# First pole tables copied within SBUF, later poles behind the first products, three groups' layer norm statistics on ScalarE

## Chip, core and metric

The kernel runs on one core of a Trainium2 chip. Its time is the device time of one execution in microseconds (us); the median of three runs is given, and one further execution was taken with the hardware profiler. The engines are TensorE (PE; its weight loads are PEld), VectorE (DVE), ScalarE (ACT), GpSimd (POOL) and SyncE (SP), which here only issues DMAs. SBUF and PSUM are the core's on-chip memories; DRAM is the chip's main memory.

## What is computed

One block with two halves. The input `x` is [2048, 576]; `c` gives six modulation rows by `silu(c) @ w_mod`. The first half is a long convolution along the sequence whose kernel comes from 576 x 128 complex poles; the second is a gated MLP with a spatial product.

```python
h = _layernorm(x) * (1 + ca) + sa
x = x + ga * _A_ref(h, A_re, A_im, B_re, B_im, C_re, C_im, log_dt, Dskip)
h = _layernorm(x) * (1 + cb) + sb
x = x + gb * _B_ref(h, w_in, w_sp, b_sp, w_out)
# in _A_ref, with dt = exp(log_dt):
P = jnp.exp((dt * (A_re + 1j * A_im))[:, :, None] * l)   # l = 0 .. 2047
K = einsum("dn,dnl,dn->dl", C, P, dt * B).real           # then FFT convolution of h with K
```

## The kernel before, in words

`ssm` is the first half, `Mlp` the second. Only the front of `ssm` is touched.

**Poles.** The powers of a pole are split into magnitude and angle. `poles(c0, c1, Q)` computes, for a chunk range of the 576 channels (chunk 0 alone, width 144, then chunks 1 to 3 together, width 432), the log magnitude per step `al`, the log weight `lw`, the angles `tau` and `tau64` and the phase `ph`. It is a generator (`run`) with five `yield`s: its caller decides when each of six segments is written out. Six products run on GpSimd (L211 to L216), the exponential, logarithms and arctangent on ScalarE, the rest on VectorE. `split3` cuts each fp32 result into three bf16 pieces that add up to it, and stores them in DRAM (`pa_d`, `pb_d`, `pc_d`). `poles_load` reads them back in another shape, 16 channels by 3 or 6 pieces on the partitions: the tables `lb` (al and lw), `lc` (tau), `la` (tau64 and ph).

**Ticks.** 36 groups of 16 channels run through a pipeline, one group a tick in a loop of 40 ticks. `e_unit` (every third tick, for three groups) multiplies `lb` with a constant selector `sel` on TensorE and takes exponentials on ScalarE (L386, L389). `t_unit` forms the angles from `lc` and `la`, rounds them with a ScalarE pass (L397) and two VectorE passes (L398, L400); `s_unit` takes sine and cosine (L405, L406); `p_unit` multiplies on VectorE two ticks after `t_unit` (L417 to L421); `kg_unit`, `d_unit` and `k1_unit` sum over the poles and transform. From tick 9 on the input side joins in: `u_load`, `u_unit`, `z_unit`, `v_unit`, and later `y_unit`. These use space that the front's pool `ep` gives back at tick 9.

**Modulation and layer norm.** `mod_load` and `mod_unit` (L312 to L324) form one modulation row each, into the tiles `gar`, `cga` and `sga` for the first half. x is handled in four groups of four blocks of 128 tokens. `ln_load` reads a group, `ln_stats` takes mean and variance with VectorE's bn_stats (L353, L354) and a reciprocal root of 11 operations of width 4 (`rsqrt`, L741 to L751), `ln_unit` normalizes one block with two VectorE passes (L363, L364), transforms it with four matmuls (L369), copies it out (L370) and stores it (L371). Two blocks are handled a tick, in ticks 0 to 7; the buffers `ln_x` are two, `st1o` two, `mpart` one.

**Order.** Instructions called through `V`, `A`, `G`, `T` and `S` are ordered for each engine by the tile framework's planner, which goes by its own estimates of when inputs are there. Calls through `mlp.tied` (class `Pin`, L132) are pinned: behind whatever was written before on the same engine. Pinning fixes the place in the engine's own order only; what is written later and is not pinned may still be moved ahead of it. All instructions pinned this way show line 132 or the line of the operation. Before the loop the loads go through a pinned `S`, in this order: poles0, c, w_mod 2, small, w_mod 1, w_mod 0, x group 0, sel, r1t 0, then, behind the first poles, their table loads, and after the first modulation units dsk, x group 1, r1t 1 and poles 1 to 3.

Of the kernel before, what the change touches and what calls it, by code (L numbers as in the profile page):

```python
# [18 lines left out]
D = 576  # L19
# [125 lines left out]
def ssm(tc, I, x1_d, consts_s, dram, mod_d, mlp):  # L145
# [5 lines left out]
    with ExitStack() as ctx:  # L151
# [26 lines left out]


        def poles(c0, c1, Q):  # L180
            w = 144 * (c1 - c0)

            def t(n, dt=F32):
                return ep.tile([128, 432], dt, name="t_" + n, bufs=1)[:, :w]

            todo = []

            def split3(src, dst, k):

                n = 3 // (c1 - c0)  # L190
                if not todo:
                    t_ = ep.tile([128, 3, 432], BF, name="pt")
                    todo.extend(t_[:, :, w * i:w * i + w] for i in range(n))
                pt = todo.pop(0)
                V.tensor_copy(pt[:, 0], src)
                q = t("sq")
                V.tensor_tensor(q, src, pt[:, 0], op=ALU.subtract)
                V.tensor_copy(pt[:, 1], q)
                V.tensor_tensor(pt[:, 2], q, pt[:, 1], op=ALU.subtract)
                for c in range(c0, c1):  # L200
                    Q.dma_start(dst[c, k:k + 3].rearrange("q (p f) -> p q f", p=128), pt[:, :, 144 * (c - c0):144 * (c - c0) + 144])

            raw = ep.tile([128, 7, w], F32, name="nat%d" % c0, bufs=1)
            for r in (slice(0, 3), slice(3, 7)):
# [3 lines left out]
            def run():  # L208
# [10 lines left out]
                V.tensor_tensor(al, dt, al, op=ALU.mult)  # L219
                split3(al, pb_d, 0)  # L220
                yield
# [18 lines left out]
                A.activation(lw, mx, AF.Ln)  # L240
                A.activation(q1, mn, AF.Square)
                A.activation(q1, q1, AF.Ln, bias=one)
                A.activation(ph, mn, AF.Arctan)
                V.scalar_tensor_tensor(lw, q1, 0.5, lw, op0=ALU.mult, op1=ALU.add)
                V.tensor_tensor(lw, lw, ldt, op=ALU.add)
                split3(lw, pb_d, 3)
                yield
# [11 lines left out]
                yield  # L259
                split3(tau, pc_d, 0)  # L260
                split3(tau64, pa_d, 0)
# [6 lines left out]
        lt = {}  # L268

        def poles_load(c, Q):  # L270
            for n, d_, k in (("lb", pb_d, 6), ("lc", pc_d, 3), ("la", pa_d, 6)):
                t_ = tb.tile([16 * k, 9, 128], BF, name=n)
                Q.dma_start(t_, d_[c].rearrange("q (c g n) -> (q c) g n", c=16, g=9))
                lt[n, c] = t_

# [71 lines left out]
        def ln_stats(i):  # L347
            x = x4s[i]
            bs = ep.tile([128, 4, 2, 6], F32, name="bs")
            mv = ep.tile([128, 4, 2], F32, name="mv")  # L350
            for b in range(4):
                for h in range(2):
                    V.bn_stats(bs[:, b, h], x[:, b, HC * h:HC * h + HC])  # L353
                V.bn_aggr(mv[:, b], bs[:, b])  # L354
            r = ep.tile([128, 4], F32, name="r")
            rsqrt(V, ep, r, mv[:, :, 1], 4)
            lns[i] = mv, r

        def ln_unit(b):
            i, j = divmod(b, 4)  # L360
            mv, r = lns[i]
            n = x4s[i][:, j]
            V.scalar_tensor_tensor(n, n, mv[:, j, 0:1], cga, op0=ALU.subtract, op1=ALU.mult)  # L363
            V.scalar_tensor_tensor(n, n, r[:, j:j + 1], sga, op0=ALU.mult, op1=ALU.add)  # L364
# [241 lines left out]
        ln_stats(1)  # L606
        sb = cs = None
        for tick in range(NG + 4):
# [1009 lines left out]
```

## Time and profile before

| | us |
|---|---|
| median of 3 runs (lowest, highest) | 1794.5 (1794.14, 1796.96) |
| profiled execution | 1798.62 |
| its span, first to last instruction | 1796.9 |
| PE, DVE, ACT, POOL busy in the span | 1695.7, 1128.8, 785.6, 224.0 |
| DVE, ACT busy from 42.5 to 161.5 us | 105.4, 82.4 |

Lines of a view read as: engine, source line, operation, tile written <- tiles read, shapes, count; then busy us, mean ns of one, and the idle time of the engine before them with what ended it ("<-DMA x" is a transfer into x, "<-ACT ft L397" ScalarE's result of line 397). In lines in order of time the first number is the start and the second the duration, in us from the span's start. "ACTq" and "SPq" are the engines' issuing of DMAs.

### The profile page before, as it was taken

The page shows a single profiled execution, that of the slowest core. Times are in us where ns is not written, and L with a number is a line of the kernel's source. Part 1 is how long each engine was busy: PE and PEld are TensorE (multiplying, and loading weights), DVE is VectorE, ACT ScalarE, POOL GpSimd, SP SyncE. Part 2 cuts the span into 40 slices and gives each one's busy share as a digit, 9 for nine tenths or more (in the row PEclk, how much of TensorE's full clock was granted, in tenths as well). Part 3 has the DMA queues.
Part 4 walks back from the last instruction along what each step waited for, and adds up shares of the span by engine and source line. Part 5 has one row for each costly group of instructions (what it writes and reads, how often), then busy time and mean ns, then how long its engine had stood idle before and what let it go on. Part 6 is the DMA issues. An engine that isn't in the chain of part 4 may idle for free.

```text
span 1796.9 us, 34078 instructions
## 1 busy us (share of the span) xinstructions
PE 1695.7 (94%) x14202; PEld 1197.6 (67%) x14202; DVE 1128.8 (63%) x2253; ACT 785.6 (44%) x1021; POOL 224.0 (12%) x350
## 2 busy tenths in 40 slices
PE   4687999996899999999999999999999999999999
PEld 1344555565455545877787777877778777887787
DVE  6987999857888997999784444474222265222322
ACT  4658999844476666555441322241111132011110
POOL 1321232342122211000000000000000000000000
PEclk8788999998899999999999999999999999999999
DMA  8457445779588788877564675562655472555520
GB/s 274 139 196 243 139 119 163 195 207 314 169 266 261 241 259 246 301 277 257 206 216 148 240 250 206 212 250 92 227 192 197 173 264 69 176 181 175 199 83 27
DMA packets 153034, 361.57 MB, mean 201 GB/s; under 512 B 24832, under 2 KB 68224, under 8 KB 150960
## 3 DMA queue, kind: packets, MB, share of 16 engines
q1 hardware_dynamic: 110272, 167.30, 29.4%
q0 software_dynamic: 33120, 153.95, 25.8%
q10 hardware_dynamic: 9488, 38.16, 5.3%
q8 instruction: 111, 1.82, 0.4%
q14 instruction: 43, 0.35, 0.1%
HBM read 256.86 MB, written 93.05 MB: 195 GB/s over the span
## 4 chain that ended last, share of the span: by engine, by line
PE 51%; DVE 16%; DMA 7%; issue 4%; ACT 4%; SPq 0%; POOL 0%; ACTq 0%; DVEq 0%; POOLq 0%
PE ps L1324 9%; PE ps L1359 8%; PE ps L1361 8%; PE ps L1360 8%; PE pz L132 3%; PE ps L1408 3%; PE ps L1409 3%; PE ps L1410 3%; DMA raw<-in_w_spT 2%; DVE zset L1066 2%; DVE gt L1373 2%; DMA z_d<-z 2%; ACT z L132 1%; DVE bsz L132 1%; PE pk L132 1%
## 5 line engine op out<-in xcount | busy, mean ns | idle before, releaser
L1359 PE MATMUL ps<-wsp,zset 128*128 128x256 f16 x2016 | 549.5, 273 | 2.8 <-DVE gt L1373 2.6
L1361 PE MATMUL ps<-wsp,zset 128*128 128x256 f16 x2016 | 549.5, 273 | 0.2 <-DVE zset L1066 0.2
L1360 PE MATMUL ps<-wsp,zset 128*128 128x256 f16 x2016 | 549.5, 273 | 0.0
L132 PE MATMUL pz<-wz,nt 128*128 128x512 f16 (+1 forms) x1120 | 227.2, 363 | 9.0 <-ACT nt L132 5.5
L1373 DVE SCALAR_TENSOR_TENSOR gt<-ps,sc,bsp 128x512 f32<-128x512 f32 x36 | 27.0, 749 | 316.1 <-PE ps L1361 316.1
L1324 PE MATMUL ps<-n2q,wf 128*128 128x512 f16 x1008 | 223.3, 379 | 0.6 <-DMA wf<-win_d 0.6
L1359 PEld LDWEIGHTS <-zset 128*128 128x128 f16 x2016 | 197.5, 98 | 29.7 <-DVE gt L1373 3.2
L1360 PEld LDWEIGHTS <-zset 128*128 128x128 f16 x2016 | 197.2, 98 | 26.1
L1361 PEld LDWEIGHTS <-zset 128*128 128x128 f16 x2016 | 197.3, 98 | 23.3 <-DVE zset L1066 0.5
L132 PEld LDWEIGHTS <-nt 128*128 128x128 f16 x1120 | 110.2, 100 | 117.4 <-ACT nt L132 7.2
L1324 PEld LDWEIGHTS <-wf 128*128 128x128 f16 x1008 | 98.6, 98 | 112.6 <-DMA wf<-win_d 1.1
L1336 POOL DMA_DIRECT2D zset<-set_d x96 | 51.1, 532 | 969.3 <-PE ps L1361 939.3
L1329 ACT ACTIVATE z<-ps,sc 128x512 f32<-128x512 f32 x56 | 37.8, 681 | 280.5 <-PE ps L1324 278.0
L1409 PE MATMUL ps<-wout,z 128*128 128x288 f16 x448 | 128.1, 286 | 0.0
L1408 PE MATMUL ps<-wout,z 128*128 128x288 f16 x448 | 128.1, 286 | 0.0
L1410 PE MATMUL ps<-wout,z 128*128 128x288 f16 x448 | 128.1, 286 | 0.0
L1373 DVE SCALAR_TENSOR_TENSOR gt<-ps,sc,gt 128x512 f32<-128x512 f32 (+1 forms) x180 | 121.9, 694 | 5.8 <-DVE gt L1373 0.5
L1066 DVE TENSOR_TENSOR zset<-raw,zset 128x1024 f16<-128x1024 f32 x48 | 58.6, 1220 | 74.7 <-ACT zset L1065 74.7
L1065 ACT ACTIVATE zset<-raw 128x1024 f16<-128x1024 f32 x48 | 50.3, 1051 | 97.5 <-PE ps L1361 70.1
L132 ACT ACTIVATE z<-pz,sc 128x512 f32<-128x512 f32 (+1 forms) x80 | 49.6, 646 | 56.8 <-DMA z_d<-z 44.4
L1418 DVE TENSOR_TENSOR ot<-ot,ps 128x288 f32<-128x288 f32 x32 | 14.2, 452 | 82.7 <-ACT ot L1417 82.7
L369 PE MATMUL ps<-ln_x,r1t 128*128 128x288 f32 x128 | 43.6, 499 | 19.0 <-issue 12.6
(311 smaller groups left out, 2827.5 us busy)
## 6 DMA issues: line engine op xcount, KB each, us to landing
zset<-set_d POOLq DMA_DIRECT2D x96, 896.0 KB, 4.9
set_d<-zset ACTq DMA_DIRECT2D x36, 896.0 KB, 5.8
raw<-z_d SPq DMA_DIRECT2D x48, 512.0 KB, 4.6
wf<-win_d SPq DMA_DIRECT2D x72, 320.0 KB, 3.4
raw<-in_w_spT SPq DMA_DIRECT2D x43, 512.0 KB, 6.0
z_d<-z POOLq DMA_DIRECT2D x32, 576.0 KB, 7.8
u_d<-st1o POOLq DMA_DIRECT2D x16, 576.0 KB, 4.5
u<-u_d SPq DMA_DIRECT2D x36, 256.0 KB, 4.8
```

Source lines behind the costliest of these rows:

```text
L132: return self.tc.keep_in_program_order(f(*a, **k))
L1065: nc.scalar.activation(o[:, k, 0], t, AF.Copy)
L1066: nc.vector.tensor_tensor(o[:, k, 1], t, o[:, k, 0], op=ALU.subtract)
L1324: nc.tensor.matmul(pm.rearrange("p (t c) -> p t c", t=4), w[:, kw], self.n2[q][:, :, kn], start=i == 0, stop=i == len(Z1) - 1)
L1336: self.nc.gpsimd.dma_start(o, self.set_d[n // 4, n % 4])
L1359: T.matmul(pm, z[:, a, 0, c], w[:, b, 0], start=i + half == 0, stop=False, skip_group_check=True)
L1360: T.matmul(pm, z[:, a, 0, c], w[:, b, 1], start=False, stop=False, skip_group_check=True)
L1361: T.matmul(pm, z[:, a, 1, c], w[:, b, 0], start=False, stop=i == 7, skip_group_check=True)
L1373: V.scalar_tensor_tensor(dst, pm, inv, to, op0=ALU.mult, op1=ALU.add)
L1408: T.matmul(pl, p[:, 1, ts], w[:, 0, hs], start=st, stop=sp)
L1409: T.matmul(pa, p[:, 0, ts], w[:, 0, hs], start=st, stop=False)
L1410: T.matmul(pa, p[:, 0, ts], w[:, 1, hs], start=False, stop=sp)
```

## The change

1. Chunk 0's pieces no longer go through DRAM. `split3` issues three DMAs for each of its five results, each of [128, 144] bf16, from SBUF straight into the table's 16 partitions. They go on pinned SP instead of ACT; the three table loads of chunk 0 are gone. The last split uses `wr` as its scratch in place of `sq`.
2. The order of loads before the loop is: poles0, c, sel, poles 1 to 3, small, w_mod 2, then the first poles with their fifteen DMAs, then w_mod 1, w_mod 0, x group 0, r1t 0, dsk, x group 1, r1t 1.
3. In the poles, the calls on VectorE, ScalarE and GpSimd are pinned for chunks 1 to 3; Square, the second Ln and Arctan are pinned for both passes, in that order. The first segment of chunks 1 to 3 is written in tick 0 in place of ahead of the loop.
4. The three modulation units of the first half and `ln_stats(0)` are written in tick 0, behind its other units; `ln_stats(1)` in tick 1. The layer norm blocks run in ticks 1 to 8.
5. Groups 1 to 3 take their sums on ScalarE: per block an Identity pass with accumulator gives the mean, and a Square pass with the negated mean as bias gives the variance.

```diff
+            V, A, G = (nc.vector, nc.scalar, nc.gpsimd) if c0 == 0 else (mlp.tied.vector, mlp.tied.scalar, mlp.tied.gpsimd)
...
-            def split3(src, dst, k):
+            def split3(src, dst, k, q=None):
...
-                q = t("sq")
+                q = t("sq") if q is None else q
...
+                if c0 == 0:
+                    t_ = dst[0]
+                    for i in range(3):
+                        o = t_[16 * (k + i):16 * (k + i) + 16].rearrange("c g n -> c (g n)")
+                        Q.dma_start(o.rearrange("c (r f) -> c r f", r=8), pt[:, i])
+                    return
...
+            pa, pb, pc = [[table(n, 0)] for n in ("la", "lb", "lc")] if c0 == 0 else (pa_d, pb_d, pc_d)
...
-                A.activation(q1, mn, AF.Square)
-                A.activation(q1, q1, AF.Ln, bias=one)
-                A.activation(ph, mn, AF.Arctan)
+                mlp.tied.scalar.activation(q1, mn, AF.Square)
+                mlp.tied.scalar.activation(q1, q1, AF.Ln, bias=one)
+                mlp.tied.scalar.activation(ph, mn, AF.Arctan)
...
-                split3(ph, pa_d, 3)
+                split3(ph, pa, 3, wr)
...
         def ln_stats(i):
             x = x4s[i]
...
+            r = ep.tile([128, 4], F32, name="r")
+            if i == 0:
...
+                lns[i] = [mv[:, b, 0:1] for b in range(4)], ALU.subtract, r
+                return
+            sums = ep.tile([128, 2, 4], F32, name="sums")
+            mean, ss = sums[:, 0], sums[:, 1]
...
             for b in range(4):
-                for h in range(2):
-                    V.bn_stats(bs[:, b, h], x[:, b, HC * h:HC * h + HC])
-                V.bn_aggr(mv[:, b], bs[:, b])
...
+                A.activation(junk(), x[:, b], AF.Identity, accum_out=mean[:, b:b + 1])
+            V.tensor_scalar(mean, mean, -1.0 / D, None, op0=ALU.mult)
+            for b in range(4):
+                A.activation(junk(), x[:, b], AF.Square, bias=mean[:, b:b + 1], accum_out=ss[:, b:b + 1])
+            V.tensor_scalar(ss, ss, 1.0 / D, None, op0=ALU.mult)
+            rsqrt(V, ep, r, ss, 4)
+            lns[i] = [mean[:, b:b + 1] for b in range(4)], ALU.add, r
...
-        p0 = poles(0, 1, A)
+        p0 = poles(0, 1, S)
         S.dma_start(cT, I["c"])
+        S.dma_start(sel, I["c_sel"])
+        p1 = poles(1, 4, mlp.tied.gpsimd)
+        S.dma_start(small, I["c_small"][:, 128:].rearrange("p (i c) -> p i c", i=6))
         mod_load(2)
-        S.dma_start(small, I["c_small"][:, 128:].rearrange("p (i c) -> p i c", i=6))
+        for _ in p0:
+            pass
+        mod_init()
         mod_load(1)
         mod_load(0)
         ln_load(0)
-        S.dma_start(sel, I["c_sel"])
         r1_load(0)
-        for _ in p0:
-            pass
-        poles_load(0, S)
-        mod_init()
-        ln_stats(0)
-        for k in (2, 1, 0):
-            mod_unit(k)
         S.dma_start(dsk, I["dsk"])
         ln_load(1)
         r1_load(1)
-        p1 = poles(1, 4, mlp.tied.gpsimd)
         S = plain
-        next(p1)
-        ln_stats(1)
...
             if tick == 0:
+                for k in (2, 1, 0):
+                    mod_unit(k)
                 mod_load(3)
+                ln_stats(0)
+            if tick == 1:
+                ln_stats(1)
...
-            j = tick
-            if j < 8:
+            j = tick - 1
+            if 0 <= j < 8:
```

More of the change, by code (lines that the diff above doesn't have):

```diff
@@ L177, in ssm, with table @@
         ep = early.enter_context(tc.tile_pool(name="ep", reuse_waits="tile", bufs=2, side="right"))
+        lt = {}
+        def table(n, c):
+            lt[n, c] = tb.tile([48 if n == "lc" else 96, 9, 128], BF, name=n)
+            return lt[n, c]
         def poles(c0, c1, Q):
             w = 144 * (c1 - c0)
+            V, A, G = (nc.vector, nc.scalar, nc.gpsimd) if c0 == 0 else (mlp.tied.vector, mlp.tied.scalar, mlp.tied.gpsimd)
             def t(n, dt=F32):
@@ L219, in run @@
                 V.tensor_tensor(al, dt, al, op=ALU.mult)
-                split3(al, pb_d, 0)
+                split3(al, pb, 0)
                 yield
@@ L240, in run @@
                 A.activation(lw, mx, AF.Ln)
-                A.activation(q1, mn, AF.Square)
-                A.activation(q1, q1, AF.Ln, bias=one)
-                A.activation(ph, mn, AF.Arctan)
+                mlp.tied.scalar.activation(q1, mn, AF.Square)
+                mlp.tied.scalar.activation(q1, q1, AF.Ln, bias=one)
+                mlp.tied.scalar.activation(ph, mn, AF.Arctan)
                 V.scalar_tensor_tensor(lw, q1, 0.5, lw, op0=ALU.mult, op1=ALU.add)
                 V.tensor_tensor(lw, lw, ldt, op=ALU.add)
-                split3(lw, pb_d, 3)
+                split3(lw, pb, 3)
                 yield
@@ L259, in run @@
                 yield
-                split3(tau, pc_d, 0)
-                split3(tau64, pa_d, 0)
+                split3(tau, pc, 0)
+                split3(tau64, pa, 0)
                 V.tensor_scalar(rnd, ph, MAGIC, MAGIC, op0=ALU.add, op1=ALU.subtract)
                 V.tensor_tensor(ph, ph, rnd, op=ALU.subtract)
-                split3(ph, pa_d, 3)
+                split3(ph, pa, 3, wr)
             return run()
-        lt = {}
         def poles_load(c, Q):
[L271 to L274, printed above, removed]
+            for n, d_ in (("lb", pb_d), ("lc", pc_d), ("la", pa_d)):
+                Q.dma_start(table(n, c), d_[c].rearrange("q (c g n) -> (q c) g n", c=16, g=9))
         ec = cp.tile([128, 5], F32, name="ec")
```

18 lines of the change are left out of this document (11 added, 7 removed).

## The prediction

> **What bounds the kernel now.** I read the page's totals first, then busy time by stretches, then the groups of the stretch that the change touches, then the order of time there.
>
> ```profile
> span 1796.9 us, 34078 instructions
> ```
>
> The profiled execution took 1798.62 us, 1.7 outside its span; the runs' median is 1794.5. The sum below is a difference made in this execution (1798.6), and I subtract it from the median.
>
> The busy time by stretches: start:end, length, then busy us of PE, PEld, DVE, ACT, POOL, clock, DMA share, GB/s.
>
> ```profile
> 21.00:31.10 10.10, 5.33 (x30) 1.94 (x28) 5.88 (x17) 2.58 (x3) 0.00 (x0) 0.94 0.81 192
> 31.10:42.50 11.40, 5.42 (x11) 1.18 (x11) 8.60 (x30) 8.71 (x10) 0.31 (x1) 0.50 0.96 360
> 42.50:161.47 118.97, 89.20 (x810) 51.48 (x813) 105.41 (x211) 82.39 (x106) 34.69 (x43) 0.82 0.51 172
> 187.89:352.90 165.01, 160.11 (x2193) 93.33 (x2195) 150.24 (x228) 154.29 (x199) 48.99 (x79) 1.00 0.55 150
> 352.90:1796.90 1444.00, 1405.41 (x10868) 1034.64 (x10860) 824.26 (x1684) 504.51 (x664) 133.80 (x212) 0.99 0.61 206
> ```
>
> From 353 us on PE is busy 97%: the change touches nothing there, and that part moves with whatever ends the front. From 188 to 353 PE, ACT and DVE are all above 90%; this too is unchanged. The front, 21 to 161 us, ends with the t_unit of tick 9. There DVE is the fullest engine: 5.88 + 8.60 + 105.41 = 119.9 of 140.5 us (85%), against 93.7 for ACT (67%) and 100 for PE (71%). So I count DVE time there, and what DVE waits for. Its groups, with busy time, mean ns, idle before and its cause:
>
> ```profile
> L353 DVE BATCH_NORM_STATS2 bs<-ln_x 128x6 f32<-128x288 f32 x32 | 12.8, 432 | 6.2 <-DMA ln_x<-in_x 6.2
> L398 DVE SCALAR_TENSOR_TENSOR ft<-ft,ps 128x1024 f32<-128x1024 f32 x9 | 10.9, 1217 | 7.7 <-ACT ft L397 7.7
> L418 DVE TENSOR_TENSOR pg<-et,ft 128x1024 f32<-128x1024 f32 x9 | 10.9, 1209 | 0.0
> L417 DVE TENSOR_TENSOR pg<-et,ft 128x512 f32<-128x512 f32 x9 | 6.2, 684 | 1.8 <-ACT ft L405 1.8
> L354 DVE BATCH_NORM_AGGREGATE mv<-bs 128x2 f32<-128x12 f32 x16 | 3.1, 195 | 0.0
> L747 DVE TENSOR_TENSOR rq<-rq,vh 128x4 f32<-128x4 f32 x12 | 1.8, 154 | 0.0
> L322 DVE SCALAR_TENSOR_TENSOR cga<-ps,gar 128x576 f32<-128x576 f32 x1 | 0.8, 757 | 3.2 <-PE ps L317 3.2
> ```
>
> DVE's 20.6 us of idle time there are ACT's tiles (7.7 + 1.8), the inputs of the layer norm (6.2), the modulation product (3.2) and small rest.
>
> **The first tables.** Now the last piece of the split is computed at 20.4, stored to DRAM, and read back (the last row is the t_unit of tick 9, which ends the front):
>
> ```profile
> 20.05 0.31 DVE L199 TENSOR_TENSOR pt<-t_sq,pt 128x144 bf16<-128x144 f32 x1
> 21.59 0.91 ACTq L201 DMA_DIRECT2D pa_d<-pt  x2
> 28.27 0.33 SPq L132 DMA_DIRECT2D lb<-pb_d  x1
> 29.64 0.30 SPq L132 DMA_DIRECT2D la<-pa_d  x1
> 31.11 1.46 PE L388 MATMUL pk<-sel,lb 96*128 96x512 bf16 x3 [3.18 <-DMA lb<-pb_d]
> 31.76 0.60 ACT L389 ACTIVATE et<-pk 128x512 f32<-128x512 f32 x1 [3.82 <-PE pk L388]
> 35.04 1.11 ACT L397 ACTIVATE ft<-ps,consts_s 128x1024 f32<-128x1024 f32 x1
> ...
> 161.47 1.11 ACT L397 ACTIVATE ft<-ps,consts_s 128x1024 f32<-128x1024 f32 x1
> ```
>
> Issue sizes and landing times of the first 45 us (KB each, median us):
>
> ```profile
> wm<-in_w_mod SPq DMA_DIRECT2D x2, 1152.0 KB, 10.8
> pb_d<-pt ACTq DMA_DIRECT2D x2, 108.0 KB, 11.7
> pa_d<-pt ACTq DMA_DIRECT2D x2, 108.0 KB, 7.5
> lb<-pb_d SPq DMA_DIRECT2D x1, 216.0 KB, 2.8
> DMA packets 4868, 12.31 MB, mean 274 GB/s; under 512 B 2491, under 2 KB 2747, under 8 KB 4099
> ```
>
> The stores take 7.5 to 11.7 us because the loads of w_mod, x and sel are in flight with them; the read, when little else is, takes 2.8. The change drops five stores and three loads and issues fifteen DMAs of 36 KB on SP, each in the written order. Ahead of them stand poles0, c, sel, poles1, small and one w_mod: by the tiles' shapes 504 + 480 + 1512 + 384 + 1296 KB, 4.3 MB, which at the mean of 274 GB/s are through at about 18 us. The other two w_mod, x and r1t cannot be issued until the last table is, so the late tables meet empty queues. At 0.35 us per issue and 2.8 us to land, the last (la) lands 3 to 4 us after 20.4, at about 24 instead of 32.4. The first t_unit then runs at about 25 to 26 instead of 35, and the exponentials, which need lb only, at about 21 to 23 instead of 31.8.
>
> *By the skill.* The Trainium skill, DMA: Bandwidth & Descriptors, section Bandwidth, asks for DMAs of 1 MiB and calls those under 64 KB descriptor-dominated, and section Anatomy of one DMA gives 2.0 us + bytes/436e3 each; an estimate by that page for fifteen of them one after the other is 31 us; the twelve that follow lw would end near 43, and the sum below would shrink to about -3. The trace does not bear this out: the reads issued at 28.27 and 29.64, 2.8 us each, were in flight together. So it gets no chance of its own.
>
> ScalarE's pinned order Ln, Square, Ln, Arctan drops the table load that now takes it back to Ln after Arctan:
>
> ```profile
> 13.13 1.28 ACT L242 ACT_TABLE_LOAD   x1
> 13.14 0.23 DVE L248 TENSOR_SCALAR t_dt<-t_dt 128x144 f32<-128x144 f32 x1 [2.08 <-ACT t_dt L243]
> ```
>
> This is 1.3 us off ACT in each of the two pole passes, so the split of lw starts sooner; DVE waited 2.1 us there, hence 0 to -2 us at the tables. I count none of it.
>
> What is late next: x for group 0, whose statistics start now at
>
> ```profile
> 25.97 1.18 DVE L353 BATCH_NORM_STATS2 bs<-ln_x 128x6 f32<-128x288 f32 x3 [1.65 <-DMA ln_x<-in_x]
> ```
>
> Its bytes (two w_mod, x, r1t: 4000 KB, 4.1 MB) start at about 21.5 and take 15 us, so it lands at 36 to 37 instead of 26. DVE's cover until then is what the early tables allow: three t_units (1.2 + 0.7 us each) and two p_units (1.2 + 4 x 0.7 us each), 13.7 us. I take that idle time in 21 to 42.5 stays at its 7 us: the early start is spent on waiting for x. Bounds: -4 (DVE's 4.2 us before 31.1 are all filled) to +9 (the rival on x).
>
> **Layer norm statistics.** Three of four groups leave DVE: three quarters of 12.8 + 3.1 us = 11.9 us. Added are two small scalings a group, like the 4-wide rows of 0.16 us: 3 x 2 x 0.16 = 0.9. Net -11.0 us of DVE. The wait for x of the later groups (from the waits after 42.5: us, times, longest) goes from DVE to ACT: -4.6 on DVE if ACT hides it, 0 if DVE then waits for ACT instead.
>
> ```profile
> DVE bs L353 <- DMA ln_x<-in_x: 4.6, 2, 2.4
> ```
>
> ACT gets, per group, four Identity and four Square passes of 576 with an accumulator read each. Rows of that width, plain and with a column as bias, and the read:
>
> ```profile
> L370 ACT ACTIVATE st1o<-ps 128x576 f32<-128x576 f32 x32 | 20.3, 648 | 20.7 <-DMA u_d<-st1o 9.8 <-PE ps L369 9.4 <-issue 1.5
> L328 ACT ACTIVATE gar<-ps,consts_s 128x576 f32<-128x576 f32 x1 | 0.7, 741 | 0.1
> L132 ACT ACTIVATION_READ_ACCUMULATOR raw<-raw 128x1 f32 x18 | 3.3, 186 | 0.0
> ```
>
> 4 x (0.65 + 0.74) + 8 x 0.19 = 7.1 us, 5.6 when neighbours overlap by 0.09; three groups 17 to 21 us. After 42.5 ACT has 119.0 - 82.4 = 36.6 us idle to take this; in a front of about 108 us it comes to (82.4 + 17 - 1.3) / 108 = 91%, as full as DVE. DVE's waits for ACT (9.5 us in rows above) will grow; from the stretch 188 to 353, where both are as full and DVE idles 14.8 of 165 us (9%), I take +5, between 0 and +16 (all ACT time unhidden).
>
> *By the skill.* The Trainium skill, ScalarE: Activation LUTs, section Rules for kernel authors, says additions and multiplications belong on VectorE rather than ScalarE; per block of 576 that agrees with the rows, 1.06 us on DVE against 1.4 to 1.8 on ACT. Taken as the whole story it makes the move a loss, which is the slower rival below.
>
> **Later poles.** GpSimd's six products run at 42 to 50 now; they slow DVE while they do:
>
> ```profile
> 44.00 1.50 DVE L219 TENSOR_TENSOR nat<-t_dt,nat 128x432 f32<-128x432 f32 x1
> 46.41 0.59 DVE L222 TENSOR_TENSOR nat<-t_dt,nat 128x432 f32<-128x432 f32 x1
> 42.19 1.28 POOL L211 TENSOR_TENSOR t_wr<-nat 128x432 f32<-128x432 f32 x1 [34.98 <-DMA nat<-in_poles]
> ```
>
> Five DVE operations lose about 0.9 us each, 4.5 in all. After the change poles1 lands by 12 us, but t_wr, one buffer, is scratch of the first poles' last split, so the products start at about 20 and slow three t_units and p_units instead: 0 (bounds -4.5, if DVE is idle then, and +1). The pass's DVE work keeps its size; pinned behind each tick's layer norm, it can wait without holding the products, which are free to pass it. The table load of the next poles stands one layer norm tick earlier on POOL:
>
> ```profile
> 156.97 1.46 PE L388 MATMUL pk<-sel,lb 96*128 96x512 bf16 x3 [3.96 <-DMA lb<-pb_d]
> ```
>
> 0 to -4, of which I count nothing, because the x of the last group ends later in the ticks and loads wait for it.
>
> **Sum.** -11.0 - 4.6 + 5 = -10.6 us at the end of the front, rounded to -10; later ticks keep their lengths. 1794.5 - 10 = 1784.5 us; this case's own range, from the bounds of ACT's cost and of the waits, is 1778 to 1790.
>
> **Rivals.**
>
> *Everything adds.* DVE reaches the 9% idle of the later ticks from the first table on: 119.9 - 11.0 = 108.9 us / 0.91 = 120 us from 24, so 144 against 161.5: -17.5, 1777 us. For it: planned work fills DVE at 91% later. Against: x comes at 37, and ACT is as full.
>
> *x paces the front.* If DVE's order puts cga, sga or the statistics of group 0 ahead of the second and third tick, DVE stands at them until 37: with only the first t_unit as cover some 9 us more idle, and -10.6 + 9 = -1.6, 1793 us. For it: the present order already put statistics ahead of work that was ready (6.2 us). Against: those waits were 2.4 us at most.
>
> *ScalarE becomes the bound (slower).* Its place is 21 to 161. ACT's idle time there is 140.5 - 93.7 = 46.8 us. If it all recurs because it is dependence and not slack, ACT needs 93.7 + 17 - 1.3 + 46.8 = 156.2, +15.7, less 8.8 us for exponentials that start at 23 instead of 31.8: +7, 1801 us. It decides when more than 40 of the 46.8 us recur. For it: statistics pass ACT, DVE, ACT, DVE, and ACT runs in order, so a late x stops exponentials. Against: at 188 to 353 ACT runs 93% full.
>
> *The pin does not hold GpSimd back.* It orders the products behind GpSimd's own work only. Should they run at 12 to 20, under the first poles, fifteen DVE operations lose 0.3 us each, as the first of these rows does beside GpSimd's work on the first poles, and the tables are 4 us later: -6, 1788.
>
> ```profile
> 6.12 0.52 DVE L225 TENSOR_SCALAR t_rnd<-nat 128x144 f32<-128x144 f32 x1
> 7.70 0.23 DVE L228 TENSOR_SCALAR t_rnd<-t_tau 128x144 f32<-128x144 f32 x1
> ```
>
> Against: t_wr, as above.
>
> **How the numbers follow.** Forecast 0.45, everything adds 0.20, x paces 0.16, ScalarE 0.14, GpSimd 0.05. About 0.2% (3.6 us) is what can be told from no change. Faster: 0.45 + 0.20 and a third of x's case and most of GpSimd's, 0.72. Same: most of x's case and edges, 0.15. Slower: 0.13, nearly all ScalarE's. The range 1770 to 1800 holds the middle cases and cuts the far ends of the fastest and the slowest.
>
> **What would show it.** L388's first matmul at 20 to 23 and L397's first at 25 to 26; no long landing of table DMAs; bn_stats eight instead of 32; the first L369 at 43 to 48; the t_unit of tick 9 near 151; ACT about 90% busy before it; the distance from there to the end unchanged within 3 us. A tick 9 at 160 with L322 or L353 waiting past 35 says x; ACT waits of DVE above 15 us say ScalarE. A changed distance after tick 9 would make the whole reckoning wrong.

## Result, and the profile after

The changed kernel took 1806.05 us (median; 1803.58 to 1807.01), the kernel before 1795.73: ratio 1.0054, 95% interval 1.0037 to 1.0072. It is slower by about 10 us where I forecast 10 us faster, and outside the range. A second measurement on another chip gave 1.0037 (1.0019 to 1.0056). The profiled execution took 1803.58 us, against 1798.62 before.

The head of the page of the kernel after, and its totals:

```profile
span 1801.8 us, 34116 instructions
...
PE 1698.7 (94%) x14202; PEld 1196.2 (66%) x14202; DVE 1116.3 (62%) x2223; ACT 802.1 (45%) x1069; POOL 222.3 (12%) x350
```

DVE lost 12.5 us of work (1128.8 to 1116.3) and ACT gained 16.5 (785.6 to 802.1), near the sum's -11.0 and +17 (for VectorE in part by luck, as e4 and e5 show). The work went where it should, and the time grew. Busy time of the front by stretches in the kernel after, with the columns of the same view before:

```profile
21.00:31.10 10.10, 6.52 (x24) 1.12 (x23) 0.00 (x0) 4.29 (x6) 4.61 (x5) 1.00 0.91 289
31.10:42.50 11.40, 8.24 (x33) 3.33 (x37) 5.14 (x7) 5.72 (x7) 0.00 (x0) 0.84 0.92 358
42.50:161.47 118.97, 92.46 (x796) 50.92 (x790) 100.14 (x215) 96.59 (x150) 26.61 (x37) 0.81 0.45 149
```

From 21 to 31 us, where DVE did 5.88 us of work before, it now does none, and from 21 to 42.5 it is idle for 16.4 of 21.5 us (7.0 before). What it waits for, by the waits of DVE from 21 to 161.5 us (us in all, times, longest):

```profile
DVE ft L424 <- ACT ft L423: 19.3, 4, 16.3
DVE sga L334 <- PE ps L327: 6.1, 1, 6.1
DVE sums L378 <- ACT mpart L377: 4.5, 2, 4.3
```

Two waits of 16.3 and 6.1 us are new. The order of time in the kernel after shows what is behind them:

```profile
17.46 3.80 SPq L132 DMA_DIRECT2D la<-pt  x6
17.77 1.44 PE L414 MATMUL pk<-sel,lb 96*128 96x512 bf16 x3 [17.77 <-DMA lb<-pt]
26.07 4.50 PE L322 MATMUL ps<-wm,ec 128*32 128x288 f32 x20 [1.11 <-ACT et L412]
31.31 2.29 PE L327 MATMUL ps<-mpart,small 128*128 128x288 f32 x4 [0.74 <-ACT mpart L324]
33.39 0.63 PE L422 MATMUL ps<-sel,la 96*128 96x512 bf16 x1
34.18 1.11 ACT L423 ACTIVATE ft<-ps,consts_s 128x1024 f32<-128x1024 f32 x1
35.32 1.22 DVE L424 SCALAR_TENSOR_TENSOR ft<-ft,ps 128x1024 f32<-128x1024 f32 x1 [16.25 <-ACT ft L423]
42.20 4.50 PE L322 MATMUL ps<-k,ec 128*32 128x288 f32 x20
49.75 0.76 DVE L334 TENSOR_TENSOR sga<-ps,gar 128x576 f32<-128x576 f32 x1 [6.08 <-PE ps L327]
50.42 1.17 DVE L365 BATCH_NORM_STATS2 bs<-ln_x 128x6 f32<-128x288 f32 x3
```

The tables are early, as forecast: lb's first product runs at 17.77 (31.11 before), and la's last piece is issued by 21.26 and has landed by 22.7. But la's product (L422) stands in TensorE's order behind modulation unit 2 (L322, L327) and runs at 33.39; the first t_unit runs at 34.18, hardly ahead of the 35.04 before. Units 1 and 0 follow one after the other; sga is there at 49.75 (29.08 before), the statistics of group 0 begin at 50.42 (25.97 before), and the first layer norm matmul runs at 64.1 us (42.6 before), the last at 159.5 (149.3 before). x of group 0 had landed at 35.3 us; it is VectorE's order that puts sga ahead of the eight statistics passes of group 0, so that DVE stands idle for 6.08 us with their input there. In the kernel before all eight ran ahead of sga. There, all three units ran between 10.93 and 28 us, while TensorE had nothing else: the tables had not landed.

The t_unit of tick 9, which I had taken for the end of the front, is at 161.60 us, 0.1 us from before; and yet the span is 4.9 us longer. Of that, 3.0 us lie between this mark and the last matmul of the pole pipeline, and 1.8 us behind that.

### The profile page after: what moved, and what is told of

The parts are those of the page before. It is cut to its first block, busy times and chain, and to the rows that moved or that the text cites. A ratio compares the mean times of both kernels' runs of the same rounds, so it can differ in the third digit from the quotient of the medians.

```text
span 1801.8 us, 34116 instructions
## 1 busy us (share of the span) xinstructions
PE 1698.7 (94%) x14202; PEld 1196.2 (66%) x14202; DVE 1116.3 (62%) x2223; ACT 802.1 (45%) x1069; POOL 222.3 (12%) x350
## 4 chain that ended last, share of the span: by engine, by line
PE 44%; DVE 15%; DMA 10%; issue 10%; ACT 3%; SPq 0%; POOL 0%; ACTq 0%; DVEq 0%; POOLq 0%
PE ps L1349 8%; PE ps L1384 8%; PE ps L1385 8%; PE ps L1386 8%; DMA z_d<-z 3%; DVE zset L1091 2%; DMA zset<-set_d 2%; PE ps L1433 2%; PE ps L1434 2%; PE ps L1435 2%; DMA raw<-in_w_spT 2%; PE pz L132 2%; DVE gt L1398 2%; DVE bsz L132 1%; ACT z L132 1%
## 5 line engine op out<-in xcount | busy, mean ns | idle before, releaser
L424 DVE SCALAR_TENSOR_TENSOR ft<-ft,ps 128x1024 f32<-128x1024 f32 x36 | 43.8, 1217 | 32.7 <-ACT ft L423 32.7
```

## Experiments

Ratios are to the kernel before on the same chip in the same session, with 95% intervals, the verdicts resting on them alone. The changed kernel itself took 1.0054 on one chip and 1.0037 on another, so ratios from different sessions are compared to no better than some 0.002. The other columns are from the one profile of each run, in us: the first t_unit, the first and the last layer norm matmul, and the last matmul of the pole pipeline (k1_unit), behind which all that the change touches has ended.

| run | ratio | first t_unit | layer norm matmuls | last k1 |
|---|---|---|---|---|
| before | 1 | 35.0 | 42.6 to 149.3 | 399.1 |
| e2, before, no units | 0.9990 (0.9971, 1.0008) | 32.7 | 40.9 to 144.8 | 393.7 |
| e5, before, statistics on ScalarE | 0.9993 (0.9975, 1.0010) | 32.1 | 37.1 to 145.1 | 392.2 |
| e12, before, pins | 1.0015 (0.9999, 1.0031) | 33.1 | 41.4 to 147.3 | 395.7 |
| e6, before, copied tables | 1.0050 (1.0031, 1.0070) | 56.3 | 62.7 to 150.7 | 400.5 |
| e1, after, no units | 0.9958 (0.9944, 0.9971) | 27.3 | 49.3 to 146.5 | 388.4 |
| e11, after, tables through DRAM | 0.9983 (0.9966, 1.0000) | 25.3 | 53.3 to 152.3 | 394.1 |
| e15, the same again | 1.0000 (0.9983, 1.0017) | 25.6 | 53.6 to 152.7 | 394.4 |
| e9, units 2, 1 ahead | 0.9991 (0.9975, 1.0007) | 31.8 | 56.4 to 151.8 | 394.9 |
| e16, after, c loaded late | 0.9998 (0.9983, 1.0012) | 27.6 | 55.4 to 151.8 | 393.8 |
| e17, DRAM and c late | 1.0008 (0.9991, 1.0024) | 26.7 | 55.7 to 151.9 | 393.4 |
| e7, units ahead, loads too | 1.0002 (0.9987, 1.0018) | 39.1 | 61.6 to 153.7 | 395.0 |
| e3, units ahead | 1.0009 (0.9986, 1.0032) | 43.8 | 61.4 to 155.7 | 398.2 |
| e14, DRAM, unit 2 ahead | 1.0018 (1.0000, 1.0036) | 29.3 | 60.8 to 155.9 | 397.3 |
| e10, unit 2 ahead | 1.0032 (1.0017, 1.0047) | 35.9 | 62.5 to 156.6 | 399.9 |
| e13, w_mod 2 late | 1.0037 (1.0020, 1.0054) | 25.0 | 59.7 to 155.9 | 397.9 |
| e18, after again | 1.0037 (1.0019, 1.0056) | 34.1 | 61.7 to 157.4 | 399.1 |
| after | 1.0054 (1.0037, 1.0072) | 34.2 | 64.1 to 159.5 | 402.2 |
| e4, after, all statistics on DVE | 1.0057 (1.0039, 1.0074) | 34.0 | 63.9 to 162.7 | 404.5 |
| e8, after, later poles not pinned | 1.0118 (1.0098, 1.0138) | 53.5 | 81.4 to 174.9 | 415.9 |

Among the runs built on the changed kernel (e1 and all below it) two things hold. From the last layer norm matmul to the last k1 it is 241.0 to 243.3 us in every one, so the layer norm's end marks the end of the front there; the t_unit of tick 9, 239.3 to 241.2 us ahead of the last k1, is as good a mark. In the runs built on the kernel before, where the layer norm is written one tick earlier, these distances are 247.1 to 249.7 and 237.1 to 238.0, so neither mark carries over from one kernel to the other without a shift. And the time follows the last k1: from e1 to e8 the last k1 moves by 27.5 us and the ratio by 0.0160, 29 us. From there to the end of the span single profiles vary between 1397.5 and 1406.3 us, with no relation to the edits; so these columns are good to some 4 us. I take the profile of before (399.1, with 1397.8 behind it) to be one with a late front and a short rest; no second profile of it was taken.

### The modulation units left out

My first theory, M: the loss is that the units now stand in the way. The rival (S in the expectations): ScalarE's statistics slow the front. e1 in the changed kernel, e2 in the kernel before:

```diff
+        for t_ in (gar, cga, sga):
+            G.memset(t_, 1.0)
+
         def mod_unit(k):
             wm = wmt.pop(k)
+            if k < 3:
+                return
```

> The changed kernel without the three modulation units of the first half: their matmuls and copies are left out, gar, cga and sga are set to one by GpSimd, their loads stay, so the first layer norm uses wrong factors. Theory M (the units, written in tick 0, stand in TensorE's order ahead of la's matmul and of each other's results, and VectorE waits 16.3 + 6.1 us for what is behind them): the first L423 falls from 34.2 to 25 or 26, the t_unit of tick 9 from 161.6 to 143 to 150, the time by 10 to 17 us against the changed kernel. Rival S (ScalarE's statistics, in order, slow the front): the t_unit of tick 9 stays within 4 us of 161.6 and the time falls by less than 5.

> The kernel before without the same three units (factors set to one, loads kept): what the units cost there. Theory M: they ran in TensorE's idle time before the first tables, so 0 to -3 us against the kernel before. If the units cost as much there as in the changed kernel (10 us or more), M falls.

Without units 2, 1 and 0 (their factors set to one, so the output is not the reference's) the changed kernel gains 0.0096 against its first measurement and 0.0079 against its second, 14 to 17 us, and ends below the kernel before; the kernel before gains 0.0010, within its uncertainty. So the same three units cost nothing that can be measured where they were, and 14 to 17 us where they are.

### Statistics alone

e4 puts the statistics of groups 1 to 3 back on VectorE in the changed kernel; e5 puts them on ScalarE in the kernel before.

```diff
-            if i == 0:
+            if i >= 0:
```

> The changed kernel with all four groups' statistics on VectorE as before. Theory M: the statistics on ScalarE were a gain in themselves, so this is 3 to 8 us slower than the changed kernel. Rival S: 5 to 10 us faster than it, at the time of the kernel before.

> The kernel before with only the statistics of groups 1 to 3 moved to ScalarE. If VectorE's time bounds the front before, as the prediction has it, 11 us of it gone give 5 to 11 us less than the kernel before. If the front is bound by chains that pass from engine to engine (the changed kernel with the statistics back on VectorE took the same time as with them on ScalarE), within 4 us of it.

1.0057 against 1.0054, and 0.9993: the move is worth nothing that can be measured either way. M had expected e4 to be 3 to 8 us slower than the changed kernel, and missed. From 21 to 161.5 us DVE is busy for 115.5 us in e5 (119.9 before) and waits for:

```profile
DVE pg L433 <- ACT ft L421: 8.5, 3, 6.0
```

The profile of e5 is one of its fastest executions (1791.46 us, its median is 1798.1) and says little on the time. What it shows is that waits for ScalarE's results come in: pg waits 8.5 us where it waited 1.8 before. In the whole kernel DVE's busy time falls by 6.6 us (1128.8 to 1122.2; from e4 to the changed kernel by 6.7, 1123.0 to 1116.3), and the time is level: its busy sum was not the bound.

### The pins

e8 takes the pins of the later poles' three engines out of the changed kernel; e12 puts the pins alone, with the first segment of the later poles in tick 0, into the kernel before.

```diff
-            V, A, G = (nc.vector, nc.scalar, nc.gpsimd) if c0 == 0 else (mlp.tied.vector, mlp.tied.scalar, mlp.tied.gpsimd)
+            V, A, G = nc.vector, nc.scalar, nc.gpsimd
```

> The changed kernel with the later poles' calls on VectorE, ScalarE and GpSimd not pinned (Square, Ln and Arctan stay pinned). Theory of the modulation units: within 4 us of the changed kernel, since their wait of 16 us is not the pin's. If the pin costs, 5 us or more less than the changed kernel; if it helps, 4 us or more above it.

> The kernel before with the pins alone: VectorE, ScalarE and GpSimd calls of the later poles and Square, Ln, Arctan of both passes pinned, the first segment of the later poles written in tick 0. If the pin is worth in the old order what it is worth in the changed one (a run of the changed kernel without it was 13 us slower), the time is 0.991 to 0.995. M says the pin only protects la's and the units' work where these come late; in the old order the tables are the last to come and the time is 0.998 to 1.002, with the first t_unit at 32 to 36 and the first layer norm matmul at 39 to 44.

e8 loses another 0.0064 (12 us). Its timeline: the later poles fill DVE ahead of everything else, and TensorE's second pair of products for the exponentials (at 41.11) waits 20.4 us for ScalarE.

```profile
24.26 0.39 DVE L246 TENSOR_SCALAR nat<-t_wr 128x432 int32<-128x432 int32 x1 [2.38 <-POOL t_wr L227]
...
50.54 0.61 DVE L206 TENSOR_TENSOR pt<-t_sq,pt 128x432 bf16<-128x432 f32 x1
54.60 1.22 DVE L424 SCALAR_TENSOR_TENSOR ft<-ft,ps 128x1024 f32<-128x1024 f32 x1 [3.45 <-ACT ft L423]
```

In the old order the pins do nothing that can be measured (1.0015). There the later poles' first product waits for its data until 42.19 us (a row of the prediction), in the changed kernel it runs at 19.15; I take that to be why the pins matter only there.

### The units written elsewhere

e3 writes the three units ahead of the loop; e7 does so and loads w_mod 1 and 0 ahead of the copies and poles 1 to 3 last; e9 and e10 write only units 2 and 1, or unit 2, ahead, load w_mod 1 early, and w_mod 0 and poles 1 to 3 behind the copies.

```diff
+        for k in (2, 1, 0):          # e9: (2, 1); e10: (2,)
+            mod_unit(k)
...
-                for k in (2, 1, 0):  # tick 0; e9: (0,); e10: (1, 0)
-                    mod_unit(k)
```

> The changed kernel with the three modulation units written ahead of the loop, behind r1_load(0); nothing else. Theory M: la's matmul no longer stands behind a unit's round trip, sga is there at 36 to 40 instead of 50.5, the layer norm's first matmul at 50 to 55 instead of 64, the time falls by 5 to 10 us against the changed kernel. Rival S: within 2 us of it. Rival X (the later landing of w_mod 1 and 0 decides): the units wait for their loads until 30 to 34, the gain is under 4.

> The changed kernel with w_mod 1 and 0 loaded ahead of the table copies, poles 1 to 3 loaded last, and the three modulation units written ahead of the loop. Theory: the changed kernel loses its gain because the transfers stand almost still from 13 to 22 us behind the table copies and the units then come late and one after the other in TensorE's order. Then sga is there at 26 to 32 instead of 50.5, the layer norm's first matmul at 36 to 44 instead of 64, the t_unit of tick 9 at 143 to 152 instead of 161.6; time 12 to 20 us less than the changed kernel, 3 to 10 less than the kernel before. If instead the pin on the later poles or the statistics on ScalarE hold the front, it stays within 5 us of the changed kernel.

> The changed kernel with modulation unit 2 and 1 written ahead of the loop and only unit 0 left in tick 0; w_mod 1 is loaded ahead of the tables and poles 1 to 3 behind x of group 0. TensorE's written order is then unit 2, unit 1, the products of lb, lc and la, unit 0. Theory M (the change lost its time because the three units stand between lb's and la's products and run one after the other until 50 us): first lb product at 25 to 27, first t_unit at 27 to 29 (34.2 in the changed kernel), the product sga at 36 to 38 (49.8), first layer norm matmul at 47 to 52 (64.1), last at 147 to 151 (159.5), time 0.996 to 0.999 of before. Rival T (the copies within SBUF themselves, by their fifteen issues and the transfers they hold back, cost the time): 1.003 or more.

> As the run before this one, but only unit 2 ahead of the loop; units 1 and 0 in tick 0. By TensorE's order unit 1 then stands between lb's and la's products, as unit 2 does in the changed kernel. M: lb's first product at 18 to 20, first t_unit 31 to 34, sga 42 to 45, first layer norm matmul 54 to 58, time between the changed kernel and the run before this, 0.998 to 1.002. T: 1.003 or more, as the run before this.

e3, e7 and e9 are all level with the kernel before, by different ways: in e3 the t_unit comes at 43.8 behind all units; in e7 sga is there at 31.6, and the t_unit at 39.1; in e9 the t_unit comes at 31.8 and sga at 39.5. So the place of the t_unit alone does not set the time: e3 has it 9.6 us later than the changed kernel. e10, where unit 1 stands between lb's and la's products as unit 2 does in the changed kernel, loses 0.0032. That fits M in kind; in size it is above the 1.002 that I had set for it, and the first layer norm matmul of e9 came at 56.4 where I expected 47 to 52. e3 and e7 missed there too (61.4 for 50 to 55, 61.6 for 36 to 44), and e7 gained 0.0035 to 0.0052 on the changed kernel, 6 to 9 us, for 12 to 20: early units alone do not bring an early layer norm.

### The tables alone

e6 puts the copies into the kernel before (on ScalarE's queue, as its stores are); e11 and e15 put chunk 0's tables through DRAM again in the changed kernel, with six stores on ScalarE's queue and three loads on SP ahead of w_mod 1, all else as changed.

```diff
-                if c0 == 0:
-                    t_ = dst[0]
...
-                    return
...
-        p0 = poles(0, 1, S)
+        p0 = poles(0, 1, A)
...
         for _ in p0:
             pass
+        poles_load(0, S)
```

> The kernel before with only chunk 0's tables copied within SBUF, fifteen DMAs on ScalarE's queue, all loads in the old order. The loads of w_mod, x and sel are in flight with them, so they land late as the stores did: tables at 26 to 29 instead of 32, time 0 to 5 us less than the kernel before. If small copies meet no such queueing, tables at 23 and 5 to 9 us less.

> The changed kernel with chunk 0's tables through DRAM again (six stores on ScalarE's queue, three loads on SP ahead of w_mod 1); everything else stays. M: the units still stand behind lb's products and now start later: first lb product 24 to 31, sga 50 to 58, first layer norm matmul 64 to 72, time 1.004 to 1.010. T: the loss goes with the copies, 0.998 to 1.002.

> The same kernel as e11_after_dram, on the chip of the two others and in five rounds. O: within 0.002 of e13_la_first. T: at least 0.004 below it.

Here theory M missed. I expected 1.004 to 1.010 of e11, since the units stay where they are; it measured 0.9983, and again 1.0000. e6, for which I had expected a gain of 0 to 5 us, loses as much as the change by the copies alone, but by another way. Its timeline shows ScalarE's queue held while it issues, and la's product behind all three units:

```profile
27.98 5.76 ACTq L210 DMA_DIRECT2D la<-pt  x5
33.79 0.65 ACT L323 ACTIVATE mpart<-ps 128x576 f32<-128x576 f32 x1 [18.86 <-DVE bs L362]
...
55.60 0.61 PE L405 MATMUL ps<-sel,la 96*128 96x512 bf16 x1
```

e11's timeline shows something else than slow copies:

```profile
21.16 0.30 SPq L132 DMA_DIRECT2D la<-pa_d  x1
23.73 0.61 PE L416 MATMUL ps<-sel,la 96*128 96x512 bf16 x1
...
27.36 4.50 PE L316 MATMUL ps<-wm,ec 128*32 128x288 f32 x20 [1.39 <-ACT et L406]
...
40.17 2.51 PE L316 MATMUL ps<-k,ec 128*32 128x288 f32 x20
```

Through DRAM la is asked for at 21.16, when the last copy is issued in the changed kernel (21.26), and lands 1.0 us after it. But la's product now stands ahead of unit 2 in TensorE's order, and the t_unit runs at 25.3. Both theories fit this run: either the copies cost time by themselves (T), or the planner, which puts each engine's instructions in order by its own estimates, takes six copies for later than one load and so places unit 2 first (O).

### The order of la's product and unit 2

Three ways to put la's product ahead of unit 2, or unit 2 out of its way. e13 loads w_mod 2 behind the copies. e16 loads c, 2.5 KB and the units' other input, behind the copies, and moves nothing else; e17 does the same with the tables through DRAM; e18 is the changed kernel on their chip. e14 has the tables through DRAM and writes unit 2 ahead of the first t_unit.

```diff
-        S.dma_start(cT, I["c"])
         S.dma_start(sel, I["c_sel"])
...
         for _ in p0:
             pass
+        S.dma_start(cT, I["c"])
         mod_init()
```

> The changed kernel with the load of w_mod 2 moved from ahead of the copies to behind them, and nothing else: TensorE's order then has la's product ahead of unit 2. Theory O (the order of la's product and unit 2 is the loss; the copies cost nothing by themselves): first lb product 17 to 19, first t_unit 25 to 27 (34.2 in the changed kernel), unit 2 at 26 to 28, sga 46 to 50, time 0.996 to 1.000 of before. Theory T (the copies cost the time): 1.003 or more in spite of an early first t_unit.

> The changed kernel with chunk 0's tables through DRAM and unit 2 written ahead of the t_unit of tick 0: unit 2's first matmuls stand ahead of lb's products, in TensorE's idle time. If the units' place is what sets the start of the layer norm: first lb product 18 to 20, t_unit 25 to 28, sga 38 to 41 (45.0 without this), first layer norm matmul 46 to 50, time 0.993 to 0.997. If the later ticks set the end of the front instead: the same 0.997 to 0.999 as without it.

> The changed kernel with the load of c (2.5 KB) moved behind the copies, and nothing else: the input of the modulation units is then late, and TensorE's order has la's product ahead of unit 2. O (the order is the loss): first t_unit 25 to 27, cga at 40 to 42, sga 44 to 46, first layer norm matmul 52 to 55, time 0.997 to 1.001 of before and at least 0.003 below the changed kernel. T (the copies cost the time): 1.003 or more, within 0.002 of the changed kernel.

> The same load of c moved, with chunk 0's tables through DRAM. O: within 0.0015 of e16_c_late, first layer norm matmul within 2 us of it. T: at least 0.003 below e16_c_late.

> The changed kernel again, on the chip of the two others: 1.004 to 1.007, first t_unit at 33 to 35, first layer norm matmul at 63 to 65.

e13 went wrong for O: 1.0037 with the t_unit at 25.0. Its timeline shows why it is no clean run: w_mod 2 is now in front of x of group 0, and of group 0's eight statistics passes one runs ahead of sga and the rest behind it. After e13's rows, the same place in e11, where all eight run ahead:

```profile
41.54 0.45 DVE L365 BATCH_NORM_STATS2 bs<-ln_x 128x6 f32<-128x288 f32 x1
45.71 0.76 DVE L334 TENSOR_TENSOR sga<-ps,gar 128x576 f32<-128x576 f32 x1 [3.71 <-PE ps L327]
46.38 0.81 DVE L365 BATCH_NORM_STATS2 bs<-ln_x 128x6 f32<-128x288 f32 x2
```

```profile
41.02 1.17 DVE L359 BATCH_NORM_STATS2 bs<-ln_x 128x6 f32<-128x288 f32 x3
44.84 0.75 DVE L328 TENSOR_TENSOR sga<-ps,gar 128x576 f32<-128x576 f32 x1
```

la's product stands ahead of unit 2 in both, at 23.8 and 23.7 us, and the three units begin within 0.6 us of each other. Yet the first layer norm matmul runs at 59.7 in e13, and at 53.3 in e11 and 53.6 in e15, which was measured on e13's chip and is 0.0037 faster. So the order of la's product and unit 2 is not the whole loss.

e16 is the cleaner run. The changed kernel with one load of 2.5 KB moved:

```profile
26.29 0.63 PE L422 MATMUL ps<-sel,la 96*128 96x512 bf16 x1
28.42 4.50 PE L322 MATMUL ps<-wm,ec 128*32 128x288 f32 x20 [1.50 <-DVE ec L294]
41.12 2.51 PE L322 MATMUL ps<-k,ec 128*32 128x288 f32 x20
41.98 1.17 DVE L365 BATCH_NORM_STATS2 bs<-ln_x 128x6 f32<-128x288 f32 x3
45.71 0.76 DVE L334 TENSOR_TENSOR sga<-ps,gar 128x576 f32<-128x576 f32 x1 [0.55 <-PE ps L327]
```

and the changed kernel itself on that chip:

```profile
25.98 4.50 PE L322 MATMUL ps<-wm,ec 128*32 128x288 f32 x20 [1.11 <-ACT et L412]
33.29 0.63 PE L422 MATMUL ps<-sel,la 96*128 96x512 bf16 x1
47.39 0.76 DVE L334 TENSOR_TENSOR sga<-ps,gar 128x576 f32<-128x576 f32 x1 [3.82 <-PE ps L327]
48.06 1.17 DVE L365 BATCH_NORM_STATS2 bs<-ln_x 128x6 f32<-128x288 f32 x3
```

0.9998 (0.9983 to 1.0012) against 1.0037 (1.0019 to 1.0056): the loss is gone although unit 2 itself begins 2.4 us later. la's product is 7.0 us earlier, and the statistics of group 0 run ahead of sga (at 41.98 instead of 48.06). So the loss goes with the order in which the planner puts the work. e17, the same through DRAM, is within 0.0010 of e16, as O said: the copies themselves cost nothing and bring nothing that can be measured.

e16 changes two orders at once, la's product and unit 2 on TensorE, and sga and the statistics on VectorE. sga itself comes at 45.71 us in e13 and in e16 alike. All eight statistics passes run ahead of sga in e11, e15, e16 and e17 (0.9983 to 1.0008); in the changed kernel, e18, e4, e10, e13 and e14 none or one does (1.0018 to 1.0057). With two or three units written ahead of the loop, in e3, e7 and e9, two or none do, and these are level as well. This points to VectorE's order, but no run changes it alone, so the shares of the two orders stay open.

e14 went wrong too: with unit 2 ahead of lb's products, the first matmuls of units 1 and 0 took 4.5 us each instead of 3.4 and 2.5 in e11, sga came at 46.9 and not at 38 to 41, and nothing was gained.

No run is measurably faster than the kernel before except e1, which leaves the units out: e11 touches it (0.9966 to 1.0000), but e15, the same kernel, took 1.0000.

## Why the prediction was wrong

**The step that is missing.** "What is late next: x for group 0" names the wrong thing. The change also moves three modulation units from ahead of the loop into tick 0; I described it in the text of the change and costed only what x does. Before, they used 17 us in which TensorE waited for tables (10.93 to 28). Afterwards, the tables are early and that gap is gone, so the units are in someone's way: unit 2 in that of la's product (DVE waits 16.3 us for it, and 6.9 us in e13, where la's product is ahead of unit 2), and unit 0 in that of group 0's statistics, which stand behind sga (6.1 us). e1 against e2 shows that the units cost this time (14 to 17 us against nothing), e16 against e18 that the loss goes with the order in which they are put (0.0039: 7 us by the ratios, 4.8 by the medians), and e17 that it is not T. How much each of the two orders takes is not shown.

**The first tables.** The landing was right: la at about 23 us where I said 24. "The first t_unit then runs at about 25 to 26" was wrong in the changed kernel (34.2), right in e13 (25.0) and nearly so in e16 (27.6): in the changed kernel la had landed by 22.7, and its product ran at 33.39, behind unit 2. Nor do the early tables need the copies: with the new order of loads, e11 has them as early through DRAM (first t_unit 25.3). The copies did overlap, as argued: la's six were issued from 17.46 to 21.26 and each landed 2.0 us after its issue.

The rate of 274 GB/s was too low: from 8 to 13 us the transfers ran at 419 GB/s, and the last of the bulk, w_mod 2, had landed by 16.2 us, not 18. And since pinned SP then waits for each table's pieces, the DMA engines idle. The stretch of 9 us in the kernel after, then in the kernel before (DMA share and GB/s are the last two columns):

```profile
13.00:22.00 9.00, 3.12 (x7) 0.78 (x8) 5.69 (x25) 3.58 (x6) 2.77 (x3) 1.00 0.47 97
```

```profile
13.00:22.00 9.00, 7.68 (x35) 2.21 (x34) 6.73 (x28) 3.60 (x6) 0.00 (x0) 1.00 1.03 307
```

**Idle time of DVE in 21 to 42.5** was to stay at 7 us, bounds -4 to +9. It became 16.4, just past the far bound, and not by x: among DVE's waits of the kernel after there is none for x. Over the whole front, 21 to 161.5 us, DVE's work fell by 14.6 us (119.9 to 105.3) and its idle time rose by as much (20.6 to 35.2), where the sum had 0.4 for the waits (-4.6 + 5). The wait for x did go (6.2 us before, none after), but the waits for ScalarE's results, taken as +5, grew by 19 us (10.2 to 29.5), 13.6 of them in the wait of the first t_unit (2.7 to 16.3).

**Layer norm statistics.** ACT's size was right (+16.5). DVE's -12.5 only looks right: by e4 and e5 the statistics are 6.6 or 6.7 us of it, where the sum had 11.0. Instructions of VectorE overlap their neighbours (L353's 32 passes of 432 ns were busy for 12.8 us, not 13.8), so taking some out saves less than their sum; whether that is the whole difference is not shown. The other 5.8 us are gone in e4 too and belong to the rest of the change. ACT's passes, in its groups from 19 to 170 us:

```profile
L380 ACT ACTIVATE mpart<-ln_x,sums 128x576 f32<-128x576 f32 x12 | 9.2, 768 | 2.5 <-DVE sums L378 2.5
L377 ACT ACTIVATE mpart<-ln_x 128x576 f32<-128x576 f32 x12 | 8.1, 678 | 0.2
L377 ACT ACTIVATION_READ_ACCUMULATOR mpart<-ln_x 128x1 f32 x12 | 2.3, 193 | 0.0
```

678 and 768 ns against the 648 and 741 of the rows I took, 193 against 186. But "So I count DVE time there" was the second step that failed. DVE's 120 of 140 us looked like a bound and was not: the statistics off it are worth 0.0003 in one order (e4 against the first measurement of the change; 0.0020 against the second) and 0.0007 in the other (e5), all within their uncertainty. DVE's work is tied to chains through ScalarE and TensorE; what it does not compute, it waits. With that fits e16, where the early t_unit and the lighter DVE both hold: it is level with the kernel before and not 10 us below it. Why the layer norm needs 92 to 99 us from its first matmul to its last in the runs of the changed kernel, and 104 to 108 in those of the kernel before (88 in e6, where it starts at 62.7), stays open.

**The end of the front.** "Ends with the t_unit of tick 9" held within the runs of one kernel, but not across the change: that mark moved by 0.1 us and the span by 4.9. I had written that a changed distance behind tick 9 would make the whole reckoning wrong, and the distance changed (1635.4 to 1640.2). Some 2 us of it are the shift between the two families of runs; "unchanged within 3 us" was also finer than one profile can tell.

**Later poles** at 0: their products did wait for t_wr (19.15 us), as argued. The pins are needed for that: without them (e8) the pass holds DVE from 24 to 51 us, and the changed kernel loses 12 us more.

**Rivals.** None had the mechanism. *ScalarE becomes the bound* had the sign and nearly the time (1801), but ACT is 76% busy from 21 to 161.5 (106.6 of 140.5), not 90%, and e4, which takes the work off it, is as slow. *x paces the front* came nearest: its sign, a tick 9 at 160 with cga or the statistics waiting past 35, did appear (161.6, with cga at 42.3 and the statistics at 50.4), and it named VectorE's order. But x had landed at 35.3 and DVE never waited for it; it waited for the units' products.

## What to carry to other kernels

Where a change fills a gap, list what ran in that gap and place it anew: work that was free there has to be paid for once its cover is gone. Where a planner orders each engine's work by estimates, the kind of a transfer (six copies or one load) or the place of one load of 2.5 KB can change the order on other engines, so read the new order there before any time is worked out from landings. The busy share of the fullest engine is no bound until a run that takes work off it has shown so.

## What the runs showed of the hardware

The same twenty matmuls of a modulation unit took from 4.50 us, in the first, ahead of which TensorE had been idle, down to 2.51 us, behind other matmuls. Stretches of the kernel before that hold one unit each (length, PE, PEld, DVE, ACT, POOL, granted clock, DMA share, GB/s):

```profile
10.93:15.43 4.50, 4.50 (x20) 0.76 (x20) 2.21 (x10) 3.63 (x5) 0.00 (x0) 1.00 1.07 329
18.39:21.42 3.03, 3.03 (x21) 0.65 (x20) 1.76 (x7) 0.65 (x1) 0.00 (x0) 1.00 1.06 329
23.39:25.90 2.51, 2.51 (x21) 0.57 (x20) 0.76 (x1) 0.00 (x0) 0.00 (x0) 1.00 1.11 244
```

The Trainium skill, TensorE: Matmul & The Clock Gate, section Part 1: The HAM clock gate, has the array at half its clock after an idle window of about 3.4 us and at the full one after as long a busy one; the ratio of the durations agrees with it (4.50 / 2.51 = 1.8), but the granted clock of these rows, 1.00 in all three, does not show it. Work just ahead is not enough: in the kernel after, unit 0 (42.20) took 4.50 us right behind 2.29 us of other matmuls, with a granted clock of 0.50. Nor does the order of the work settle it: unit 1 of the changed kernel took 3.01 us in its first profile (34.34) and 4.50 in e18 (34.24). In e14 units 1 and 0 took 4.50 us each, 3.1 us more together than in e11, which is most of the 3.4 us by which unit 1 began earlier there.

A DMA of 36 KB within SBUF landed 2.0 us after its issue when the bulk of the loads was through, and 6.9 us (median of lb's six) behind the bulk of the loads, from the issues of the kernel after to 40 us:

```profile
lb<-pt SPq DMA_DIRECT2D x6, 36.0 KB, 6.9
la<-pt SPq DMA_DIRECT2D x6, 36.0 KB, 2.0
```
